# Attention units with one gate each: a gate's copies behind the next scores, ranking from unit 19, matmuls of ones moved

## The chip, the cores and the metric

The kernel runs on one core of a Trainium2 chip. The time is device time in microseconds (us) of one execution. The kernel before was run three times: median 845.96 us, lowest 845.76, highest 846.55. One execution was profiled; it took 846.0 us, of which the profile's span is 844.2.

Engines are called by the profile's names: PE (TensorE) for matmuls and PEld for its loads of weights, DVE (VectorE), ACT (ScalarE), POOL (GpSimd), and SP (SyncE), which issues most transfers.

## What is computed

Three layers follow each other. Attention over 4 x 8 heads of 576 positions and 64 columns, where the first four heads see the last 32 positions and the other four every fourth of the last 128. Then a mixture of 8 experts over the 2304 tokens, of which each token takes two, chosen by noisy gates. Then a last layer shared by all tokens.

```python
scores = scale * np.matmul(q, k.transpose(0, 1, 3, 2))
attn = softmax(np.where(masks, scores, -1e9))
x = np.matmul(attn, v)                                   # 2304 x 512
logits = x @ w_gate
noisy_logits = logits + np.log1p(np.exp(x @ w_noise)) * noise
top2 = the two largest of noisy_logits, weights by their softmax
out[mask] += top2_w * (np.maximum(x[mask] @ w1[e], 0) @ w2[e])
h = out @ w_in;  solu = h * softmax(h)
return (layer_norm(solu) * g_ln) @ w_out
```

## The kernel before

**Attention in units.** The attention is cut into 24 units (NG), numbered s. Unit s belongs to pair p = s // 3 of heads, and t = s % 3 is its third of the positions. A unit handles two pairs of heads, h = 0 and 1, with three blocks each. The work of one unit's group passes through five functions:

- scores(s), lines 168 and 175: on PE the mask and then the products of queries and keys into two banks of PSUM, tags "s" and "t", of two buffers each.
- soft_a(s), lines 184 to 188: on DVE the negative maxima (tile ng), on ACT six exponentials (tile p) that also give the sums.
- soft_b(s), lines 195 to 199: on DVE one over the sums (tile r), on POOL the scaled p (tile pn).
- ptrans(s), lines 208 to 212: on PE six transposes of pn into PSUM of tag "p" (two buffers, one for each h), and copies to SBUF (tile ptS). The copy of h = 0 is ACT's; that of h = 1 is DVE's while s is below PD = 12, then ACT's too.
- pv(s), line 227: on PE the products with v (tag "v", one buffer). What it returns, evac (lines 233 and 236), copies the result on DVE to xt, the transposed input of the next layer.

**The loop over units** (lines 842 to 897) writes the order of every engine's queue by hand, because each engine runs its instructions in the order in which they are issued here. Unit s issues, in this order: the left-over copies of the unit before (`late`), soft_a(s + 1), soft_b(s), the copies of pv(s - 3), scores(s + 2), loads of keys and queries, ptrans(s - 1), pv(s - 2), the loads of v, what `fill` holds for this unit, the gates of this unit, a piece of the splitting of weights (a cast on ACT, line 508, and a difference on POOL, line 511), and a piece of the routing of tokens.

**Gates.** gate(n), lines 258 to 279, takes 128 tokens of xt. On PE it transposes them back to rows and computes their logits in the same matmuls (line 262), into PSUM ga_a and ga_b, which both have tag "p" and so take both of its buffers (or "s" and "t" where it is told so). It returns evac: on DVE the sum of the logits (lines 273 and 274, tile ga), on ACT two copies of the rows (lines 275 and 276, tile xo), and a store of the rows to DRAM (xs, line 277, on SP's queue). GS says which gates a unit has; GE does it for units 24 and 25. The copies of gates 5, 7, 9 and 11 are issued at once, those of the others go to `late` and are issued first in the next unit. A gate can only run when its tokens' xt is complete. Gates 16 and 17 stand behind the loop.

**Routing.** front(s0, n0, n1) computes on DVE, with one exponential on ACT (line 299), the noisy logits of tokens' tiles n0 to n1 and the two largest. rank(n0, n1, ...) counts by matmuls how many tokens come ahead for an expert (lines 343 and 345), and from these builds the lists of tokens of each expert: wide tables (tile hot, line 391 on DVE, multiplied on POOL at line 393), small tables (line 399 on DVE), and matmuls of both into ixp (line 404). From ixp comes idx (lines 411 and 412), and then `then()` is called: early() gathers the first expert's tokens (line 524, an indirect transfer that POOL issues).

front and rank are generators. They yield a planner's cost in nanoseconds after each piece, and wait in the list bg:

```python
    at(FA, lambda: bg.append(front(0, 0, 4)))
    at(FB, lambda: bg.extend((front(0, 4, N1), rank(0, N1, 9, 3, early))))
    at(FC, lambda: bg.append(front(N1, N1, N2)))
```

Up to unit FB - 1 each unit takes three pieces. From FB to unit 23 it takes pieces up to PT = 2000 ns by the planner's costs (a negative cost ends it). Behind the loop come gates 16 and 17, pieces up to 740 ns, the copies of these two gates, and then drain(), which issues all that is left. Only then the transposes of the gathered rows (xtrans, line 541) and the first expert's matmuls (l1, line 554) follow.

**Matmuls of ones.** heat(n), lines 837 to 840, issues n matmuls of a tile of ones whose result nobody reads, into a buffer of tag "p".

Of the kernel before, what the change touches and what calls it, by code (L numbers as in the profile page):

```python
# [34 lines left out]
H0, H1 = 34, 20  # L35
# [4 lines left out]
M1 = 1  # L40
SH = 17
M2 = 6
GS = {8: (0,), 9: (1,), 10: (2,), 11: (3,), 14: (5, 6), 15: (7, 8), 16: (4,), 20: (9, 10), 21: (11, 12)}
FA, FB, FC = 12, 17, 22
WP, WG = (8, 9, 10), 11
CEV = True
GE = (((13, "p", "p"), (14, "s", "t")), ((15, "s", "t"),))
# [59 lines left out]
def tile_kernel(ctx, tc, kq, vw, gates_w, noise, w1, w2, w_in, w_out, g_ln, masks, cpack, out, stop=None):  # L107
# [39 lines left out]
    def load_kq(j, u0=0, u1=S):  # L147
        o = j * 128 * 2 * S
        dst = KQ[j % 4][:, W:].rearrange("p (a s) -> p a s", a=2)[:, :, u0:u1]
        nc.sync.dma_start(dst, dram_ap(kq, o + u0, [[2 * S, 128], [S, 2], [1, u1 - u0]]))  # L150

    def load_v(b, d):
        o = (2 * b + d) * 64 * NBLK * 4 * D
        nc.sync.dma_start(VW[d][W:].rearrange("p i h d -> p (i h d)"),
                          dram_ap(vw, o, [[NBLK * 4 * D, 64], [1, NBLK * 4 * D]]))
# [6 lines left out]
    def scores(s):  # L162
        p, t = divmod(s, 3)
        ps = [psum.tile([128, 3, 96], F32, name="s", tag="st"[h]) for h in range(2)]
        half = [slice(64 * h, 64 * h + 64) for h in range(2)]
        for l in half:
            for h, hd in enumerate(half):
                nc.tensor.matmul(ps[h][l], idb[hd, hd], mk[hd, p % 2, 3 * t:3 * t + 3, :], start=True, stop=False,
                                 skip_group_check=True)
        for i in range(3):  # L170
            u = 64 * (3 * t + i)
            for c, l in enumerate(half):
                j = (2 * p + c) % 4
                for h, hd in enumerate(half):
                    nc.tensor.matmul(ps[h][l, i], QT[j][hd, u:u + 64], KT[j][hd, u:u + 96], start=False,
                                     stop=i == 2, skip_group_check=True)
        G[s] = {"s": ps}

    def soft_a(s):
        ng = work.tile([128, 2, 3], F32, name="ng", bufs=3)  # L180
        p = work.tile([128, 2, 3, 96], F32, name="p", bufs=2)
        sm = work.tile([128, 2, 3], F32, name="sm", bufs=3)
        for h in range(2):
            nc.vector.tensor_reduce(out=ng[:, h], in_=G[s]["s"][h], axis=AX.X, op=OP.max, negate=True)  # L184
        nc.vector.tensor_scalar(ng, ng, scale, None, op0=OP.mult)
        for h in range(2):
            for i in range(3):
                nc.scalar.activation(p[:, h, i], G[s]["s"][h][:, i], AF.Exp, scale=scale, bias=ng[:, h, i:i + 1],  # L188
                                     accum_out=sm[:, h, i:i + 1])
        G[s].update(p=p, sm=sm)  # L190

    def soft_b(s):
        p = G[s]["p"]
        r = work.tile([128, 2, 3], F32, name="r", bufs=3)
        nc.vector.tensor_scalar(r, G[s]["sm"], 1e-9, None, op0=OP.add)  # L195
        nc.vector.reciprocal(r, r)
        pn = work.tile([128, 2, 3, 96], F32, name="pn", bufs=2)
        for h in range(2):
            nc.gpsimd.tensor_tensor(pn[:, h], p[:, h], r[:, h, :, None].to_broadcast([128, 3, 96]), op=OP.mult)
        G[s]["pn"] = pn  # L200

    def ptrans(s):
        pn = G[s]["pn"]
        t = work.tile([96, 2, 3, 128], F32, name="ptS", bufs=2)
        for h in range(2):
            ps = psum.tile([96, 3, 128], F32, name="pt", tag="p")
            for i in range(3):
                nc.tensor.transpose(ps[:, i], pn[:, h, i], idf)
            if h and s < PD:
                nc.vector.tensor_copy(t[:, h], ps)  # L210
            else:
                nc.scalar.copy(t[:, h], ps)
        G[s]["pt"] = t

    def pv(s):
        p, t = divmod(s, 3)
        b, k = divmod(p, 2)
        pt = G[s]["pt"]
        if b not in XT:
            XT[b] = big.tile([128, 4, S], F32, name="xt", tag="xt", bufs=2)  # L220
        x = XT[b][:, 2 * k:2 * k + 2]
        full = psum.tile([128, 512], F32, name="pv", tag="v", bufs=1)
        ps = full[:, :384].rearrange("p (c u) -> p c u", c=2)
        for c in range(2):
            for i in range(3):
                for h in range(2):
                    nc.tensor.matmul(ps[64 * h:64 * h + 64, c, 64 * i:64 * i + 64], VW[k][:, 3 * t + i, 2 * c + h, :],  # L227
                                     pt[:, h, i, 64 * c:64 * c + 64], start=True, stop=True, skip_group_check=True)
        del G[s]

        def evac():
            if k:
                nc.vector.tensor_copy(x[:, :, 192 * t:192 * t + 192], ps)
                return
            for c in range(2):
                nc.vector.tensor_copy(x[:, c].rearrange("p (c i) -> p c i", c=DIL)[:, :, 48 * t:48 * t + 48],
                                      ps[:, c].rearrange("p (i c) -> p c i", c=DIL))

        return evac
# [24 lines left out]
    def gate(n, ta="p", tb="p"):  # L264
        pa = psum.tile([128, 3, 144], F32, name="ga_a", tag=ta)
        pb = psum.tile([128, 1, 144], F32, name="ga_b", tag=tb)
        gate_mm(n, 0, 3, pa)
        gate_mm(n, 3, 4, pb)

        def evac():  # L270
            xo = work.tile([128, DM], F32, name="xo", tag="y", bufs=3)
            t = work.tile([128, 16], F32, name="gt")
            nc.vector.reduce_sum(t, pa[:, :, 128:].rearrange("p k e -> p e k"), axis=AX.X)
            nc.vector.tensor_add(ga[:, n], t, pb[:, 0, 128:])
            nc.scalar.copy(xo[:, :384].rearrange("p (k d) -> p k d", k=3), pa[:, :, :128])
            nc.scalar.copy(xo[:, 384:], pb[:, 0, :128])
            nc.sync.dma_start(xs[128 * n:128 * n + 128], xo)

        return evac
# [472 lines left out]
    def pump(n=1):  # L752
        t = 0
        for _ in range(n):
            while bg:
                try:
                    t = next(bg[0]) or 0
                    break
                except StopIteration:
                    bg.pop(0)  # L760
        return t

    def pump_t(t, stop=False):
        while bg and t > 0:
            c = pump()
            t -= abs(c)
            if stop and c < 0:
                break
        return t
# [67 lines left out]
    def heat(n):  # L837
        ps = psum.tile([128, 128], F32, name="heat", tag="p")
        for _ in range(n):
            nc.tensor.matmul(ps, one, one, start=True, stop=True, skip_group_check=True)  # L840

    heat(H0)
    scores(0)
    soft_a(0)
    scores(1)
    heat(H1)
    late = []
    debt = 0
    for s in range(NG + 2):
        p, t = divmod(s, 3)  # L850
        for f in late:
            f()
        late = []
        if s + 1 < NG:
            soft_a(s + 1)
        if s < NG:
            soft_b(s)
        if s > 2:
            pve()
        if s == 1:  # L860
            ptrans(0)
        if s + 2 < NG:
            scores(s + 2)
        if s == 0:
            heat(H1)
        if t == 0 and p + 2 < 8:
            load_kq(2 * p + 4)
            load_kq(2 * p + 5)
        if 1 < s <= NG:
            ptrans(s - 1)  # L870
        if s > 1:
            pve = pv(s - 2)
            if s == NG + 1:
                pve()
        b, k = divmod(s - 5, 6)
        if s > 4 and k % 3 == 0 and b < 3:
            load_v(b + 1, k // 3)
        for f, a in fill.get(s, []):
            f(*a)
        tiles = [(n,) for n in GS.get(s, ())] + (list(GE[s - NG]) if s >= NG else [])  # L880
        for a in tiles:
            f = gate(*a)
            if a[0] in (5, 7, 9, 11):
                f()
            else:
                late.append(f)
        if s >= WG and first:
            try:
                next(first[0])
            except StopIteration:  # L890
                first.pop(0)
        if FB <= s < NG:
            debt = pump_t(PT + min(debt, 0), True)
        elif s < FB:
            pump(3)
    for h in late:
        h()
    late = [gate(16), gate(17, "s", "t")]
# [222 lines left out]
```

## Time and profile before

| | |
|---|---|
| median of three runs | 845.96 us (845.76 to 846.55) |
| the profiled execution | 846.0 us, span 844.2 us, mean granted clock 0.967 |
| PE busy | 794.4 us, 94% of the span |
| PEld busy | 697.7 us, 83% |
| DVE busy | 519.1 us, 61% |
| ACT busy | 322.7 us, 38% |
| POOL busy | 194.5 us, 23% |

A granted clock of 1.00 is 2.4 GHz on PE, and 0.50 is 1.2 GHz. A mean between them belongs to a stretch that had both. Idle time in front of an instruction is given with what ended it ("<-").

### The profile page before, as it was taken

How to read it: one execution, taken by the hardware profiler on the slowest of the kernel's cores; microseconds unless marked ns; L12 is line 12 of the kernel's file. 1: busy time of each engine (PE TensorE's matmuls, PEld its weight loads, DVE VectorE, ACT ScalarE, POOL GpSimd, SP SyncE). 2: the span in 40 equal slices, each digit the busy share in tenths (PEclk: the TensorE clock that was granted, in tenths of full speed). 3: DMA queues.
4: the chain of work that ended last, by engine and by line, in shares of the span. 5: the costliest groups of instructions: out<-in, count | busy, mean ns of one | idle time of the engine just before them, and what ended most of it. 6: DMA issues, size and time to landing. Idle time of an engine off the chain costs nothing.

```text
span 844.2 us, 14236 instructions
## 1 busy us (share of the span) xinstructions
PE 794.4 (94%) x5470; PEld 697.7 (83%) x5470; DVE 519.1 (61%) x1213; ACT 322.7 (38%) x821; POOL 194.5 (23%) x202
## 2 busy tenths in 40 slices
PE   6977766799999999999999999999999999999997
PEld 5766656798988989989989889899887888888886
DVE  3865576535655845755757554432566777877783
ACT  4877633233322433323223323332434443344332
POOL 3664551812011011010010110022224312322200
PEclk8999757899999999999999999999999999999999
DMA  7666213336336445455264463352422222212101
GB/s 258 215 229 216 88 51 114 112 106 191 119 125 192 158 156 169 150 175 179 97 200 150 137 193 107 118 156 67 145 76 77 67 70 75 63 51 76 38 25 41
DMA packets 56729, 106.21 MB, mean 126 GB/s; under 512 B 6096, under 2 KB 26576, under 8 KB 56144
## 3 DMA queue, kind: packets, MB, share of 16 engines
q1 hardware_dynamic: 50576, 85.31, 31.0%
q0 software_dynamic: 6080, 19.93, 8.0%
q8 instruction: 45, 0.74, 0.4%
q14 instruction: 28, 0.23, 0.1%
HBM read 81.03 MB, written 24.19 MB: 125 GB/s over the span
## 4 chain that ended last, share of the span: by engine, by line
PE 82%; DVE 6%; ACT 1%; DMA 1%; issue 1%; POOL 0%; DVEq 0%; ACTq 0%
PE l L554 53%; PE fh L688 12%; PE fo L554 11%; PE xtp L541 2%; PE fzp L706 2%; PE ga_a L262 1%; DVE hot L399 1%; PE xtp L626 1%; DVE hot L391 1%; ACT p L188 1%; DMA xg<-xs,idx 1%; DVE ng L184 1%; PE ixp L404 0%; PE pv L227 0%; DVE r L195 0%
## 5 line engine op out<-in xcount | busy, mean ns | idle before, releaser
L524 POOL DMA_INDIRECT xg<-xs,idx x40 | 46.2, 1154 | 338.3 <-PE xtp L541 326.0
L554 PE MATMUL l<-x,w1h 128*128 128x256 f32 x512 | 96.8, 287 | 0.8 <-ACT x L545 0.7
L554 PE MATMUL l<-x1h,w1h 128*128 128x384 f32 x256 | 85.9, 335 | 0.0
L554 PEld LDWEIGHTS l<-x,w1h 128*128 128x128 f32 x512 | 84.1, 195 | 2.1 <-ACT x L545 1.1
L554 PE MATMUL l<-x1l,w1h 128*128 128x384 f32 x256 | 85.8, 335 | 0.0
L554 PE MATMUL l<-x1h,w1l 128*128 128x384 f32 x256 | 85.6, 334 | 0.0
L554 PE MATMUL l<-w2h,h1h 128*128 128x512 f32 x192 | 76.8, 400 | 0.0
L554 PE MATMUL l<-w2h,h1l 128*128 128x512 f32 x192 | 75.1, 391 | 0.0
L554 PE MATMUL l<-w2l,h1h 128*128 128x512 f32 x192 | 74.9, 390 | 0.0
L554 PE MATMUL l<-x,w1l 128*128 128x256 f32 x256 | 73.5, 287 | 0.0
L575 DVE SCALAR_TENSOR_TENSOR h1l<-l,h1h 128x384 fp32r<-128x384 f32 x64 | 35.4, 553 | 46.9 <-ACT h1h L574 46.6
L574 ACT ACTIVATE h1h<-l 128x384 fp32r<-128x384 f32 x64 | 31.5, 493 | 83.2 <-PE l L554 81.6
L511 DVE TENSOR_TENSOR w1l<-raw,w1h 128x1024 fp32r<-128x1024 f32 x32 | 38.3, 1230 | 28.2 <-ACT w1h L508 28.2
L600 DVE COPY yo<-l 128x512 f32<-128x512 f32 x22 | 15.2, 691 | 64.6 <-PE l L554 64.6
L188 ACT ACTIVATE p<-s,ng 128x96 f32<-128x96 f32 x144 | 47.0, 345 | 18.6 <-DVE r L195 18.4
L554 PE MATMUL fo<-w2x,fz 128*128 128x512 f32 (+1 forms) x228 | 52.8, 379 | 0.0
L554 PE MATMUL l<-w2h,h0h 128*128 128x512 f32 x128 | 51.9, 405 | 0.0
L554 PE MATMUL l<-w2h,h0l 128*128 128x512 f32 x128 | 51.1, 399 | 0.0
L554 PE MATMUL l<-w2l,h0h 128*128 128x512 f32 x128 | 50.9, 398 | 0.0
L598 ACT COPY yo<-l 128x512 f32<-128x512 f32 x18 | 10.6, 588 | 104.3 <-PE l L554 100.7
L688 PE MATMUL fh<-w1h,fx 128*128 128x512 f32 x144 | 49.1, 403 | 1.2 <-ACT fx L632 0.7
L620 POOL TENSOR_TENSOR yg<-yg 128x512 f32<-128x512 f32 x18 | 23.3, 1293 | 116.2 <-ACT yg L619 116.2
(198 smaller groups left out, 1921.8 us busy)
## 6 DMA issues: line engine op xcount, KB each, us to landing
raw<-in_moe_w_dram SPq DMA_DIRECT2D x64, 512.0 KB
ys<-yo SPq DMA_DIRECT2D x40, 256.0 KB
kq<-in_kq_dram SPq DMA_DIRECT2D x14, 576.0 KB
vwt<-in_vw_dram SPq DMA_DIRECT2D x8, 576.0 KB
xs<-xo SPq DMA_DIRECT2D x18, 256.0 KB
out_dram<-yo SPq DMA_DIRECT2D x17, 256.0 KB
raw<-in_moe_w_in_dram SPq DMA_DIRECT2D x8, 512.0 KB
raw<-in_moe_w_out_dram SPq DMA_DIRECT2D x8, 512.0 KB
```

Source lines behind the costliest of these rows:

```text
L188: nc.scalar.activation(p[:, h, i], G[s]["s"][h][:, i], AF.Exp, scale=scale, bias=ng[:, h, i:i + 1], accum_out=sm[:, h, i:i + 1])
L511: (eng or nc.vector).tensor_sub(l, r, h.bitcast(F32))
L524: nc.gpsimd.indirect_dma_start(out=t, out_offset=None, in_=xs[:128 * N1] if h == 0 else xs, in_offset=bass.IndirectOffsetOnAxis(ap=idx[:, ...
L541: nc.tensor.transpose(ps[:, kk], t[:, 128 * kk:128 * kk + 128], idf)
L554: nc.tensor.matmul(ps, A[x], Bm[y], start=first and i == 0, stop=last and i == 2)
L574: nc.scalar.activation(hh[:, ft], ps, AF.Relu)
L575: nc.vector.scalar_tensor_tensor(hl[:, ft], ps, 0.0, hh[:, ft].bitcast(F32), op0=OP.max, op1=OP.subtract)
L598: nc.scalar.copy(y, ps)
L600: nc.vector.tensor_copy(y, ps)
L620: nc.gpsimd.tensor_tensor(a, a, b, op=OP.add)
L688: nc.tensor.matmul(ps, FX[n][x][:, kk], W1[y][:, 2 * c:2 * c + 2, kk], start=kk == 0 and i == 0, stop=kk == 3 and i == 2)
L706: nc.tensor.transpose(ps[:, kk], u[:, c, 128 * kk:128 * kk + 128], idf)
```

## The change

GS gives every unit from 14 to 18 and from 20 to 23 one gate, where four units had two; gate 4 moves from unit 16 to unit 18. FA, FB and FC, the units at which the pieces of the routing enter the list, move from 12, 17 and 22 to 13, 19 and 24. All copies of gates go to `late`, and `late` is issued behind scores(s + 2) instead of at the head of the unit. Of the three sets of matmuls of ones the second one moves ahead of scores(1), and the third, in unit 0, goes.

```diff
-GS = {8: (0,), 9: (1,), 10: (2,), 11: (3,), 14: (5, 6), 15: (7, 8), 16: (4,), 20: (9, 10), 21: (11, 12)}
-FA, FB, FC = 12, 17, 22
+GS = {8: (0,), 9: (1,), 10: (2,), 11: (3,), 14: (5,), 15: (6,), 16: (7,), 17: (8,), 18: (4,), 20: (9,), 21: (10,), 22: (11,),
+      23: (12,)}
+FA, FB, FC = 13, 19, 24
...
     heat(H0)
     scores(0)
     soft_a(0)
+    heat(H1)
     scores(1)
-    heat(H1)
     late = []
     debt = 0
     for s in range(NG + 2):
         p, t = divmod(s, 3)
-        for f in late:
-            f()
-        late = []
         if s + 1 < NG:
             soft_a(s + 1)
...
         if s + 2 < NG:
             scores(s + 2)
-        if s == 0:
-            heat(H1)
+        for f in late:
+            f()
+        late = []
...
         for a in tiles:
             f = gate(*a)
-            if a[0] in (5, 7, 9, 11):
-                f()
-            else:
-                late.append(f)
+            late.append(f)
```

## Rows read from the trace of the kernel before

**Rows 1.** Stretches: start:end, us, busy of each engine (instructions), granted clock, DMA share, GB/s.

```profile
11.04:13.63 2.59, 2.59 (x40) 2.36 (x40) 1.06 (x4) 0.00 (x1) 0.00 (x0) 0.50 1.03 421
40.74:58.54 17.80, 14.18 (x259) 11.40 (x256) 11.27 (x39) 12.69 (x62) 9.52 (x12) 1.00 0.86 286
58.54:61.42 2.88, 1.94 (x53) 1.55 (x53) 2.75 (x9) 2.78 (x15) 2.37 (x4) 1.00 0.00 0
61.42:93.48 32.06, 22.61 (x396) 18.10 (x394) 22.45 (x102) 22.16 (x100) 18.16 (x21) 0.99 0.46 150
83.47:93.48 10.01, 5.81 (x119) 4.28 (x117) 9.47 (x40) 6.15 (x31) 7.16 (x8) 0.96 0.16 49
93.48:109.99 16.51, 12.73 (x128) 11.12 (x129) 7.20 (x36) 9.42 (x40) 4.88 (x6) 0.71 0.32 115
109.99:132.44 22.45, 16.42 (x188) 14.22 (x187) 14.53 (x31) 7.76 (x26) 11.60 (x10) 0.63 0.26 75
132.44:140.70 8.26, 2.80 (x17) 2.00 (x16) 5.89 (x39) 2.50 (x7) 2.10 (x2) 0.77 0.60 188
140.70:844.20 703.50, 691.56 (x3798) 612.26 (x3798) 431.47 (x883) 240.20 (x444) 126.06 (x113) 0.99 0.37 116
```

**Rows 2.** Order of time, unit 10: start, us, engine, line, what, count, idle and releaser.

```profile
40.74 0.34 ACT L188 ACTIVATE p<-s,ng 128x96 f32<-128x96 f32 x1 [0.63 <-DVE r L195]
...
42.66 0.48 ACT L212 COPY ptS<-pt 96x384 f32<-96x384 f32 x1
...
43.39 0.21 DVE L273 TENSOR_REDUCE gt<-ga_a 128x16 f32<-128x48 f32 x1 [1.48 <-PE ga_a L262]
...
43.83 0.81 DVE L184 TENSOR_REDUCE ng<-s 128x3 f32<-128x288 f32 x2
...
44.95 0.34 ACT L188 ACTIVATE p<-s,ng 128x96 f32<-128x96 f32 x1 [0.67 <-DVE r L195]
```

**Rows 3.** Order of time, unit 2 to 3: transposes, DVE's copy, next maxima.

```profile
19.43 0.86 PE L208 MATMUL pt<-cp,pn 128*96 128x128 f32 x6
...
20.33 0.55 DVE L210 COPY ptS<-pt 96x384 f32<-96x384 f32 x1 [0.67 <-PE pt L208]
...
20.81 0.81 DVE L184 TENSOR_REDUCE ng<-s 128x3 f32<-128x288 f32 x2
```

**Rows 4.** Order of time, unit 14 to 15: two gates.

```profile
65.15 0.48 ACT L275 COPY xo<-ga_a 128x384 f32<-128x384 f32 x1 [0.96 <-DVE gt L273]
...
65.69 1.00 PE L262 MATMUL ga_a<-wg,xt 128*128 128x144 f32 x6 [0.56 <-ACT xo L275]
...
66.86 0.32 PE L168 MATMUL s<-mk 64*64 64x288 bf16 x4
```

**Rows 5.** Order of time, unit 12 to 13: first front's exponential read, then pv.

```profile
56.45 1.07 DVE L301 TENSOR_SCALAR rw<-ru 128x32 f32<-128x32 f32 x1 [1.36 <-ACT ru L299]
...
59.23 0.92 PE L227 MATMUL pv<-ptS,vwt 96*64 96x64 f32 x24 [2.17 <-DVE xt L233]
```

**Rows 6.** Order of time, unit 20: pv behind the second front.

```profile
94.18 1.55 PE L227 MATMUL pv<-ptS,vwt 96*64 96x64 f32 x24 [3.06 <-DVE xt L233]
```

**Rows 7.** Lines 391 and 399 (min/median/max ns), then the index in order of time.

```profile
L391 DVE TENSOR_TENSOR hot<-cp,pbi x5: 642/1335/1735, 111.1 to 157.2; 128x288 f16<-128x288 f32 x3, 128x720 f16<-128x720 f32 x2
...
L399 DVE TENSOR_TENSOR hot<-cp,pbi x9: 344/901/1415, 114.0 to 160.4; 128x192 f16<-128x192 f32 x6, 128x384 f16<-128x384 f32 x3
...
121.12 1.43 PE L404 MATMUL ixp<-hot 128*64 128x40 f16 x24 [0.99 <-DVE hot L399]
...
131.75 0.19 DVE L411 TENSOR_SCALAR ix<-ixp 128x40 f32<-128x40 f32 x1
```

**Rows 8.** Order of time, units 0 and 1: scores 1, ones, group 2's exponentials.

```profile
11.04 0.46 PE L168 MATMUL s<-mk 64*64 64x288 bf16 x4 [5.16 <-DMA mk<-in_masks_dram]
...
12.39 2.08 PE L840 MATMUL heat<-one 128*128 128x128 bf16 x20
...
16.59 0.34 ACT L188 ACTIVATE p<-s,ng 128x96 f32<-128x96 f32 x1 [0.92 <-DVE r L195]
```

## The prediction

> **What bounds the kernel now.** I read the table of stretches first, then the instructions in order of time inside the stretches that stood out, then the single lines of the ranking. I cut the stretches at the first exponential of a group of scores: group g's exponentials are issued in unit g-1, so group 10's stand in unit 9. In [rows 1] the 703.50 us from 140.70 on have TensorE busy for 691.56 of them: the experts and the last layer are TensorE's own, and the change touches nothing there. Everything it touches lies ahead of that, where no engine is full. There I call the time from one group's first exponential to the next group's a round; a round without a gate is 2.88 us (58.54 to 61.42 [rows 1]).
>
> Why a round with a gate is longer shows in [rows 2]: exponentials at 40.74, the copy of the transposes at 42.66 (1.92 later), DVE's read of the gate at 43.39 after 1.48 us idle for its matmuls, and only then the next maxima at 43.83 (0.44 later) and the next exponentials at 44.95. The gate's reads stand ahead of the next group's maxima on DVE and of its exponentials on ACT, so one round takes 4.21 us. Two gates in a unit are worse: the second one's matmuls start 0.54 us after the first one's copy does [rows 4].
>
> **The change, part by part.** All sums are against the profiled execution, 846.0 us (span 844.2 and 1.8 around it), 0.04 above the median of the runs shown.
>
> *Matmuls of ones.* TensorE's queue holds 34 at the start, 20 between scores 1 and scores 2, and 20 more behind those; after the change 34, and 20 where TensorE waits anyway (5.16 us idle before scores 1 [rows 8]). So scores 2 no longer stand behind 2.08 us of ones. Group 2's exponentials start at 16.59; ACT is through with group 1's at 13.63 + 1.92 = 15.55 (13.63 is a cut of [rows 1]), so at most 1.0 is gained. The other bound is a loss: scores 1 run at 1.2 GHz now, and with nothing behind them the clock may stay there for the next two units; doubling the 0.86 us of a set of transposes [rows 3] is the nearest price, and half of it hidden gives 0.4 lost. I take 0.2 gained. From 11.04 to 13.63 the granted clock is 0.50, 1.2 GHz [rows 1], after those 5.16 us without a matmul. The Trainium skill (TensorE: Matmul & The Clock Gate, "Why this matters for your kernels") tells kernels to leave no idle gaps between bursts of matmuls, or the rate halves. By that rule, with which this row agrees, the moved ones, which end well ahead of scores 1, would not save the clock; the 0.2 would be a loss and the sum 0.4 higher.
>
> *Copies behind the next scores, gates 0 to 3.* Round 9 to 10 loses its gate (4.21 to 2.88); unit 8's copy to xstr stays in DVE's queue ahead of the next maxima, so I take 1.1 of the 1.33. The next four rounds get a new loop. A gate's two results take both banks of tag "p", which the next transposes want. Those now wait for the copies, the copies stand behind the exponentials on ACT, and up to PD = 12 the second copy of the transposes is DVE's, ahead of the next maxima in its queue. The loop: maxima to exponentials 1.12 (43.83 to 44.95 [rows 2]), exponentials 1.92, copy of the gate to TensorE 0.54 [rows 4], transposes to DVE's copy 0.90, that copy to the next maxima 0.48 [rows 3]; together 4.96, where it was 4.21. Four of them are 19.84; from group 10 to 14 it was 17.80 [rows 1]. That is 2.0 lost.
>
> *The first front, one unit later.* Its first exponential on ACT makes DVE wait, and the maxima behind it. Before, that is in round 13 to 14: 17.80 less three rounds of 4.21 and one of 2.88 leaves 2.29; the reading of ACT's result took 1.07 us on DVE at 56.45 [rows 5]. It moves to round 14 to 15, which was 2.88: 2.3 lost there (what it cost before is inside the 17.80). Up to group 15, then, 1.1 gained and 4.3 lost: **3.2 lost**.
>
> *One gate a unit, gates 5, 6, 7, 8, 4.* Groups 15 to 21 took 32.06 us [rows 1]. Now there is one round without a gate (3.5: 2.88 and something for the second half of xstr in unit 14) and five with one. The copy of h = 1 is ACT's there, so DVE is out of the loop, and the round's lower bound is ACT's own: 1.92 + 0.54 + 0.90 + 0.48 for the last copy = 3.84. The upper bound is the loop above, 4.96. I take the middle, 4.4, because ACT also has a cast of a weight in most of these units. 3.5 + 22.0 = 25.5: **6.6 gained**. TensorE needs about 3.65 a round (0.7 for scores, half of the 1.35 from 11.04 to 12.39 at half rate [rows 8]; 0.86 for transposes, 0.92 for pv, 1.17 for a gate from 65.69 to 66.86 [rows 3 to 5]), so it nearly fills it.
>
> *Groups 21 to 23.* These held two units of two gates at half clock: 16.51 us at a mean clock of 0.71. The planner's numbers put into these two units (20 and 21) the same eight and nine steps of the front that units 18 and 19 have now, and those took 10.01 us [rows 1] with no gates. One gate's read on DVE (0.44 [rows 2]) comes on top: 10.4, **6.1 gained**.
>
> *From group 23 to the first gather.* This is 22.45 us now, with the tables for the index (lines 391, 399) inside, at a mean clock of 0.63 [rows 1]. Ranking begins two units later, so by the planner's costs unit 23 gets as far as unit 21 did, and the tables fall behind the last gates: one in the step of 740 ns before gates 16 and 17 are read, the rest in drain(). TensorE's list before that: three sets of transposes, four of pv, gates 11 to 15: 3 x 0.86 + 4 x 0.92 + 5 x 1.17 = 12.1 us at full clock. It starts 2.5 us after group 23's exponentials do (1.92 + 0.54), and I add 1.5 for waits on copies: 16.1. In the round before that, TensorE waits some 3 us for DVE's front, as it did at 94.18 (3.06 us idle, and pv then took 1.55 instead of 0.92 [rows 6]); so I expect 1.2 GHz for a stretch here and add 2.5 (bounds 0 and 5.1; the 16.51 us at 0.71 hold 9.6 us at half rate, which lose 4.8). So 18.6. Then gates 16 and 17, 2.3, and their read, 0.4; the second wide table 1.3 (line 391's median); six small ones; the last 24 index matmuls 1.4; from ix to the gather 0.7 (131.75 to 132.44) [rows 1, 7]. A small table took 0.34 to 1.42, median 0.90 [rows 7]; POOL, which had transposes' inputs and weights to make beside them, has little more than its multiplications now, so I take 0.55 (3.3; bounds 2.1 and 5.4). In sum 28.0: **5.6 lost**. Here row and rule can be weighed: the row only shows the spread. The Trainium skill (SBUF — State Buffer, "Who interferes with whom") says that DVE with two operands in SBUF and a reading POOL hold a shared port by turns for a whole instruction. By it four of the six would run bare, at 0.34, and the sum be about 0.8 lower.
>
> *Behind it.* The 8.26 us from gather to the experts' first matmul, and all after that, carry over. DMA queues: SP gets the same transfers in the same order; a store of a gate stands ahead of kq's loads as before, 2 us later, and those have four units to land. POOL's order is the same but for the tables' multiplications, which move ahead of the first gather; priced above.
>
> Sum: -0.2 + 3.2 - 6.6 - 6.1 + 5.6 = -4.1, so **841.9 us**.
>
> **The rivals.** *A, the clock holds after group 22* and POOL leaves the tables alone: 2.5 and 1.2 less, 838.2. For it: gates no longer come in pairs. Against it: the front's steps are the same, and they starved TensorE before [rows 6].
>
> *B, the loop through the two banks everywhere.* If a round costs the whole loop also in units 15 to 19, because TensorE, let go late by the banks, has the next scores late, five rounds cost 4.96 (2.8 more), and gates 10 to 12 0.55 each: 4.4 more, 846.3, no change. The change then doesn't do what it says: the wait for a gate is moved to the banks, not removed. For it: TensorE's 3.65 leaves little slack. Against: ACT makes both copies there, so DVE's maxima needn't wait for the transposes.
>
> *C, the clock falls at unit 13's wait.* Round 14 to 15 is 5.2 us with 2.5 of TensorE's work (3.65 less a gate), so it waits 2.7. Before, a wait of 2.17 in such a round left the clock at 1.00 [rows 1, 5], and one of 3.06 stands where pv next ran slow [rows 6]; 2.7 lies between. Rounds of 7.3 (twice 3.65) then replace 4.4 for as long as it lasts. Over 9.6 us at half rate that is 1.3 rounds in place of 2.2, 3.8 lost, no change in all; over 16.6 (as in the 22.45 at 0.63) it is 6.6 lost, **848.5**, slower. It decides from about 15 us on.
>
> **How the numbers follow.** A difference under 0.2% (1.7 us) can't be told from no change. Chances: the forecast 0.51 (839.5 to 844.2), A 0.19, B 0.14, C 0.16. So faster 0.70, same 0.14, slower 0.16. The range is 836.5 to 848.5: low end A with rounds near 3.84, high end C's whole price.
>
> **What would show it.** Right: exponentials of groups 17 to 21 some 4.4 us apart; groups 10 to 14 about 5.0 apart, with DVE's copy of h = 1 just ahead of the maxima; group 23 near 99; lines 391 and 399 behind the last gate, TensorE idle beside them; first gather near 127, experts' first matmul near 136. Wrong: rounds of 5 in units 15 to 19, a stretch at 1.2 GHz around 65 to 85, or an index table that takes over 6 us.

## The result, and the profile after

The changed kernel took 838.22 us (median of four runs, 837.50 to 839.57) beside 845.86 us for the kernel before in the same job (four runs, 843.23 to 846.55): a ratio of 0.9917, 95% interval 0.9893 to 0.9942. That is 7.6 us faster by the medians. The forecast was 841.9, 4.1 faster.

The profiled execution of the changed kernel took 839.57 us, the longest of its four; its span is 837.8. The two profiled spans differ by 6.4 us, and this is the difference that can be followed from stretch to stretch. The lines of the kernel quoted here stand one higher in the changed kernel than before. First the stretches, cut at the same events as in [rows 1] (columns: start:end, us, busy of PE, PEld, DVE, ACT and POOL with their instructions, granted clock, DMA share, GB/s):

```profile
39.04:59.82 20.78, 15.60 (x287) 13.15 (x280) 10.26 (x39) 13.28 (x62) 9.52 (x12) 0.92 0.64 212
59.82:64.99 5.17, 3.33 (x64) 2.44 (x61) 3.25 (x8) 2.90 (x16) 3.58 (x4) 1.00 0.51 184
64.99:90.89 25.90, 22.16 (x370) 18.77 (x374) 20.68 (x77) 21.77 (x100) 15.85 (x20) 0.87 0.55 185
90.89:100.62 9.73, 6.77 (x125) 5.78 (x118) 9.08 (x43) 7.24 (x32) 6.05 (x7) 0.96 0.44 143
100.62:127.34 26.72, 20.66 (x229) 17.92 (x227) 15.37 (x56) 11.08 (x37) 10.25 (x10) 0.76 0.34 119
127.34:134.26 6.92, 2.18 (x9) 1.44 (x9) 5.36 (x35) 1.40 (x3) 2.10 (x2) 0.50 0.31 81
134.26:837.80 703.54, 691.59 (x3798) 612.22 (x3798) 431.59 (x883) 239.78 (x444) 125.92 (x113) 0.99 0.36 116
```

| stretch | before | after | difference | forecast |
|---|---|---|---|---|
| start to group 10 | 40.74 | 39.04 | -1.70 | -1.3 |
| groups 10 to 14 | 17.80 | 20.78 | +2.98 | +2.0 |
| groups 14 to 15 | 2.88 | 5.17 | +2.29 | +2.3 |
| groups 15 to 21 | 32.06 | 25.90 | -6.16 | -6.6 |
| groups 21 to 23 | 16.51 | 9.73 | -6.78 | -6.1 |
| group 23 to the first gather | 22.45 | 26.72 | +4.27 | +5.6 |
| gather to the experts' first matmul | 8.26 | 6.92 | -1.34 | 0 |
| from there to the end | 703.50 | 703.54 | +0.04 | 0 |
| sum | 844.20 | 837.80 | -6.40 | -4.1 |

What was gained, 12.9 us in the units that had two gates, was partly given back in three places. Each can be seen.

**Given back: rounds 10 to 14.** The order of time in one such round of the changed kernel (start, us, engine, line, operation, tile, count, idle before and what ended it):

```profile
54.62 0.34 ACT L189 ACTIVATE p<-s,ng 128x96 f32<-128x96 f32 x1 [0.86 <-DVE r L196]
...
56.54 0.50 ACT L276 COPY xo<-ga_a 128x384 f32<-128x384 f32 x1
...
57.18 0.83 PE L209 MATMUL pt<-cp,pn 128*96 128x128 f32 x6 [1.41 <-ACT xo L276]
...
58.05 0.55 DVE L211 COPY ptS<-pt 96x384 f32<-96x384 f32 x1 [2.39 <-PE pt L209]
...
58.53 0.81 DVE L185 TENSOR_REDUCE ng<-s 128x3 f32<-128x288 f32 x2
...
59.82 0.34 ACT L189 ACTIVATE p<-s,ng 128x96 f32<-128x96 f32 x1 [1.05 <-DVE r L196]
```

Read it as a chain. The copy of the gate stands behind the exponentials (54.62 to 56.54), TensorE's transposes wait for it (57.18, released by xo), DVE's copy waits for the transposes (58.05, after 2.39 us idle), the maxima stand behind that copy (58.53), and the next exponentials behind them. One turn is 5.20 us where [rows 2] had 4.21. Over the attention units the view of tile xo's waiters has "PE pt L209" 11 times, 12.8 us in all.

**Given back: the first front's wait**, in round 14 to 15:

```profile
62.47 0.26 ACT L300 ACTIVATE ru<-ra 128x32 f32<-128x32 f32 x1
...
62.76 1.21 DVE L302 TENSOR_SCALAR rw<-ru 128x32 f32<-128x32 f32 x1 [1.85 <-ACT ru L300]
...
64.99 0.34 ACT L189 ACTIVATE p<-s,ng 128x96 f32<-128x96 f32 x1 [2.27 <-DVE r L196]
...
65.68 1.12 PE L228 MATMUL pv<-ptS,vwt 96*64 96x64 f32 x16 [2.16 <-DVE xt L234]
```

DVE waits 1.85 us for one small exponential, the maxima wait behind it, and TensorE then waits 2.16 us (the last row shows 16 of this pv's 24 matmuls). What follows is the low clock of rival C, for a short time: 0.60 from 64.99 to 73.44, then 1.00 to 90.89.

**Gained: one gate a unit.** A round of the changed kernel with the gate's copies and both copies of the transposes on ACT:

```profile
77.55 0.34 ACT L189 ACTIVATE p<-s,ng 128x96 f32<-128x96 f32 x1
...
79.46 0.50 ACT L276 COPY xo<-ga_a 128x384 f32<-128x384 f32 x1
...
79.75 0.80 DVE L185 TENSOR_REDUCE ng<-s 128x3 f32<-128x288 f32 x2
...
80.11 0.83 PE L209 MATMUL pt<-cp,pn 128*96 128x128 f32 x6 [0.53 <-ACT xo L276]
...
80.71 0.85 ACT L213 COPY ptS<-pt 96x384 f32<-96x384 f32 x2 [0.57 <-PE pt L209]
...
81.45 0.62 ACT L509 CAST w1h<-raw 128x512 fp32r<-128x512 f32 x1
...
81.97 0.34 ACT L189 ACTIVATE p<-s,ng 128x96 f32<-128x96 f32 x1
```

Here DVE's maxima start at 79.75, long before they are needed. ACT sets the round: exponentials 1.91, the gate's copies and the wait for the transposes 1.25 (79.46 to 80.71), their copies 0.74, the cast of a weight 0.52; together 4.42. The rounds from group 17 to 21 are 4.11, 4.42, 4.41 and 4.51. Before, the two rounds between groups 21 and 23, with two gates each and more than half of the time at the low clock, hold 16.51 us [rows 1]. The other two rounds with two gates, groups 15 to 17 of the kernel before, ran at a granted clock of 1.00 and took 6.83 and 6.82 us. So the pair of gates is dear without the low clock too; up to 2.9 of the 16.51 us go with the front's waits and the low clock, which no run takes apart.

**Given back: the tables behind the last gates.** From the last gates to the experts:

```profile
121.20 1.38 DVE L392 TENSOR_TENSOR hot<-cp,pbi 128x720 f16<-128x720 f32 x1
...
122.51 2.88 DVE L400 TENSOR_TENSOR hot<-cp,pbi 128x192 f16<-128x192 f32 x6
122.67 1.44 POOL L394 TENSOR_TENSOR hot<-hot,cp 128x720 f16<-128x720 f16 x1 [0.84 <-DVE hot L392]
...
124.37 2.24 PE L405 MATMUL ixp<-hot 128*64 128x40 f16 x33 [1.20 <-DVE hot L400]
...
126.65 0.20 DVE L412 TENSOR_SCALAR ix<-ixp 128x40 f32<-128x40 f32 x1 [1.17 <-PE ixp L405]
...
127.34 1.16 POOL L525 DMA_INDIRECT xg<-xs,idx  x1 [3.24 <-DVE ef L419]
...
131.08 1.09 PE L542 MATMUL xtp<-cp,xg 128*128 128x128 f32 x4 [4.47 <-DMA xg<-xs,idx]
...
132.49 1.09 PE L542 MATMUL xtp<-cp,xg 128*128 128x128 f32 x4 [0.32 <-DMA xg<-xs,idx]
```

From 121.01, when gates 16 and 17 have left TensorE, to 127.34 it has nothing to do but the index.

### The profile page after: what moved, and what is told of

Read it like the earlier page. It is cut to its first block, busy times and chain, and to the rows that moved or that the text cites. A ratio compares the mean times of both kernels' runs of the same rounds, so it can differ in the third digit from the quotient of the medians.

```text
span 837.8 us, 14196 instructions
## 1 busy us (share of the span) xinstructions
PE 793.7 (95%) x5450; PEld 697.8 (83%) x5450; DVE 519.3 (62%) x1213; ACT 321.7 (38%) x821; POOL 193.0 (23%) x202
## 4 chain that ended last, share of the span: by engine, by line
PE 87%; DVE 6%; ACT 3%; DMA 1%; issue 1%; SPq 1%; POOL 0%; DVEq 0%; ACTq 0%
PE l L555 53%; PE fh L689 12%; PE fo L555 11%; ACT p L189 3%; PE xtp L542 2%; PE fzp L707 2%; PE pt L209 2%; PE ga_a L263 1%; DVE ng L185 1%; DMA mk<-in_masks_dram 1%; PE pv L228 1%; PE xtp L627 1%; PE s L176 1%; DVE hot L400 1%; DVE hot L392 1%
```

## The experiments

Ten kernels ran, each timed in five rounds against the kernel before on the same chip. "Experts" is the start of the experts' first matmul in the profile; behind it the ten profiles and the two above take 701.9 to 703.6 us whatever the kernel, so a single profile is best compared there. Two kernels of one job can be compared by their medians. The changed kernel ran in another job than the ten: the kernel before had a median of 845.86 us there and of 844.03, 844.43 and 844.96 in the jobs of e1 to e4, e5 to e8, and e9 and e10. So a difference of 1 or 2 us from the changed kernel is given by the ratios too (times 845 us).

| kernel | median us (range, runs) | ratio to before (95%) | experts |
|---|---|---|---|
| before | 845.86 (843.23 to 846.55, 4) | | 140.70 |
| changed | 838.22 (837.50 to 839.57, 4) | 0.9917 (0.9893 to 0.9942) | 134.26 |
| e1_heat_back | 838.15 (836.49 to 839.77, 6) | 0.9924 (0.9907 to 0.9942) | 134.37 |
| e2_copies_first | 837.55 (835.69 to 838.64, 6) | 0.9914 (0.9896 to 0.9931) | 133.53 |
| e3_pd8 | 835.89 (834.67 to 837.03, 5) | 0.9895 (0.9878 to 0.9911) | 131.66 |
| e4_stop | 836.65 (834.37 to 839.41, 6) | 0.9905 (0.9884 to 0.9926) | 132.41 |
| e5_tables_24 | 835.16 (833.49 to 835.26, 5) | 0.9885 (0.9868 to 0.9903) | 128.13 |
| e6_before_rank19 | 843.25 (841.29 to 844.36, 12) | 0.9980 (0.9968 to 0.9991) | 137.88 |
| e7_all | 829.67 (827.60 to 831.46, 5) | 0.9818 (0.9796 to 0.9839) | 126.17 |
| e8_hybrid | 828.90 (827.84 to 830.12, 5) | 0.9810 (0.9793 to 0.9827) | 125.08 |
| e9_hybrid_heat | 828.63 (826.13 to 830.06, 5) | 0.9795 (0.9774 to 0.9816) | 124.01 |
| e10_no_heat1 | 840.55 (837.62 to 841.44, 6) | 0.9933 (0.9914 to 0.9952) | 136.34 |

### The matmuls of ones put back (e1_heat_back)

```diff
     soft_a(0)
-    heat(H1)
     scores(1)
+    heat(H1)
...
             scores(s + 2)
+        if s == 0:
+            heat(H1)
```

> The changed kernel with its matmuls of ones put back as before (20 behind scores 1, 20 behind scores 2). My theory, that the order of gates makes the gain and the head next to nothing: 838.0 to 839.2 us, group 2's exponentials later by up to 1.0 us against the start of scores 1, rounds from group 9 on as in the changed kernel. Rival, that the moved matmuls of ones keep TensorE's clock up and make much of the gain: 840 us or more, with a clock of 0.5 for longer up to group 10.

838.15 beside 838.22 (by the ratios 0.6 more): no difference that can be told. The rounds from group 10 to 14 are 5.01, 5.02, 5.01 and 5.23, at a granted clock of 1.00, and the transposes and pv in them take 0.83 and 0.92 us each time. So the longer rounds are not the clock's doing, and the rival, 840 us or more, falls: much of the gain is not in the order of the ones. Less than about 2 us of it isn't excluded by the intervals.

### The copies back at the head of the unit (e2_copies_first)

```diff
         p, t = divmod(s, 3)
+        for f in late:
+            f()
+        late = []
...
             scores(s + 2)
-        for f in late:
-            f()
-        late = []
```

> The changed kernel with the gates' copies back at the head of the unit, still one gate a unit. My theory, that behind the exponentials the copies cost rounds 10 to 14 (5.2 us where they were 4.2) and save in rounds 16 to 23: rounds 10 to 13 back at 4.2 (3 us gained), rounds of gates from 16 on near 5.0 (the one single gate with ACT making both copies took 5.0 before; 3 to 4 us lost), in sum 838 to 840. Rival, that the order of the copies is the whole gain: 844 to 846.

837.55, no slower than the changed kernel, and far from the rival's 844 to 846. From group 10 to 13 the old order is faster, 4.19 a round against 5.0 to 5.6 (round 9 to 10 is slower, 4.86 against 3.67). Behind group 16 it is slower: 5.29, 5.00, 5.30 and 4.99 where the changed kernel has 5.29, 4.11, 4.42 and 4.41; only the last round to group 21, left without a gate's copies by the old order, is shorter, 2.94 against 4.51. In sum groups 9 to 14 take 20.32 us here and 24.45 in the changed kernel, groups 14 to 21 34.51 and 31.07, groups 21 to 23 10.87 and 9.73. One such round of this kernel, in order of time:

```profile
71.68 0.34 ACT L189 ACTIVATE p<-s,ng 128x96 f32<-128x96 f32 x1 [0.63 <-DVE r L196]
...
74.12 1.00 PE L263 MATMUL ga_a<-wg,xt 128*128 128x144 f32 x6 [0.76 <-ACT ptS L213]
...
75.16 0.21 DVE L274 TENSOR_REDUCE gt<-ga_a 128x16 f32<-128x48 f32 x1 [0.67 <-PE ga_a L263]
...
75.56 0.82 DVE L185 TENSOR_REDUCE ng<-s 128x3 f32<-128x288 f32 x2
...
76.68 0.34 ACT L189 ACTIVATE p<-s,ng 128x96 f32<-128x96 f32 x1 [0.63 <-DVE r L196]
```

The gate waits for the copies of the transposes, which hold its banks (74.12); DVE reads it ahead of the maxima (75.16, 75.56). So each order has its own loop. Where the copy of h = 1 is DVE's, the old loop of 4.19 is the shorter one; where both copies are ACT's, the new order is, 4.4 against 5.0. Over the attention the two balance (65.70 and 65.25 us from group 9 to 23), so the order of the copies is not the gain of the whole change. That is left to what this kernel keeps: one gate a unit, with the later ranking (e6).

### Both copies of the transposes on ACT from unit 8 (e3_pd8)

```diff
-PD = 12
+PD = 8
```

> The changed kernel with PD = 8 in place of 12: ACT, not DVE, makes the copy of the second half of the transposes in units 9 to 12. My theory, that these rounds are a loop through that copy in DVE's queue: rounds 10 to 14 fall from about 5.2 to 4.2 to 4.6, 835.5 to 836.5 us. Rival, that the wait for the two banks of tag p sets the round whoever makes the copy: rounds stay at 5.0 and the time at 838.2.

835.89, 2.3 less than the changed kernel, and 2.3 less than e1 of the same job (1.9 by the ratios, whose intervals overlap). Groups 10 to 14 take 17.83 us in place of 20.78, or of e1's 20.27. Their rounds are 3.90, 5.12, 4.40 and 4.41; the second, at a mean granted clock of 0.67, lies outside the 4.2 to 4.6 expected. A round at the full clock:

```profile
47.59 0.35 ACT L189 ACTIVATE p<-s,ng 128x96 f32<-128x96 f32 x1
...
49.91 0.82 DVE L185 TENSOR_REDUCE ng<-s 128x3 f32<-128x288 f32 x2 [0.52 <-PE s L176]
50.13 0.83 PE L209 MATMUL pt<-cp,pn 128*96 128x128 f32 x6 [0.29 <-ACT xo L276]
...
51.99 0.34 ACT L189 ACTIVATE p<-s,ng 128x96 f32<-128x96 f32 x1
```

The maxima (49.91) now come before the transposes (50.13), and what they wait for is their scores. The round is 4.40, ACT's own bound as in units 17 to 19. The loop through DVE's copy is confirmed.

### A waiting piece ends the unit's share (e4_stop)

```diff
         elif s < FB:
-            pump(3)
+            for _ in range(3):
+                if pump() < 0:
+                    break
```

> The changed kernel where a piece of the first front that waits for ACT ends the unit's share (as it does from unit 19 on), so that DVE's read of ACT's exponential stands in the next unit. My theory, that round 14 to 15 holds a 2.3 us stall of DVE behind that exponential: that round falls from 5.2 to 3.0 to 3.4 and the time to 836.0 to 836.8 us. Rival, that the stall only moves to the next unit, where DVE is as short of time: 838.0.

836.65, 1.6 less (1.0 by the ratios, whose intervals overlap): the time alone doesn't show a gain, the round does. The front's pieces with a negative cost, which wait for ACT, now end a unit's share ahead of FB too, as they already did behind it. In order of time around group 15 of this kernel:

```profile
60.21 0.81 DVE L185 TENSOR_REDUCE ng<-s 128x3 f32<-128x288 f32 x2
...
61.85 0.25 ACT L300 ACTIVATE ru<-ra 128x32 f32<-128x32 f32 x1
62.09 0.34 ACT L189 ACTIVATE p<-s,ng 128x96 f32<-128x96 f32 x1
...
63.38 0.64 DVE L302 TENSOR_SCALAR rw<-ru 128x32 f32<-128x32 f32 x1
```

The maxima (60.21) precede the exponential (61.85), and DVE reads it a unit later without waiting. Round 14 to 15 is 2.89 in place of 5.17, and the granted clock is 1.00 from 62.09 to 87.35. In e1, e3 and e10, which keep the wait (2.15, 2.21 and 2.17 us), it is 0.59 to 0.60 from group 15 to 17, as in the changed kernel, and in e5 (2.17 us) 0.78. So in these kernels the wait of TensorE at this place and the lower clock behind it go together.

### The tables also in units 24 and 25 (e5_tables_24)

```diff
-        if FB <= s < NG:
+        if FB <= s < NG + 2:
             debt = pump_t(PT + min(debt, 0), True)
```

> The changed kernel that also lets units 24 and 25 take pieces of the ranking (2000 ns each by the planner's costs), so that the tables of the index stand beside the last gates in place of behind them. My theory, that the tables behind the last gates cost the 4.3 us that group 23 to the first gather got longer: the gather comes 2 to 4 us earlier and the time is 834.5 to 836.5 us, although the copies of gates 13 to 15 are then late. Rival, that DVE's tables only push those copies and pv back by as much: 837.5 to 838.5.

835.16, 3.1 less (2.7 by the ratios). The order of time in this kernel:

```profile
111.27 1.73 DVE L392 TENSOR_TENSOR hot<-cp,pbi 128x720 f16<-128x720 f32 x2
...
112.91 1.55 DVE L400 TENSOR_TENSOR hot<-cp,pbi 128x192 f16<-128x192 f32 x1
...
117.04 1.42 DVE L400 TENSOR_TENSOR hot<-cp,pbi 128x192 f16<-128x192 f32 x5
...
120.00 1.15 POOL L525 DMA_INDIRECT xg<-xs,idx  x1 [3.06 <-DVE ef L419]
...
126.37 1.08 PE L542 MATMUL xtp<-cp,xg 128*128 128x128 f32 x4 [1.70 <-DMA xg<-xs,idx]
```

The tables stand among the last transposes and gates, and the gather starts 21.4 us after group 23 (98.59) in place of 26.7. Of these 5.3 us 1.2 are given back: from the gather to the experts it is 8.13 us again, not 6.92. The second gather's rows come 4.90 us after its issue at 121.47 here, 3.68 in the changed kernel (128.81 to 132.49).

### Later ranking alone, in the kernel before (e6_before_rank19)

```diff
-FA, FB, FC = 12, 17, 22
+FA, FB, FC = 13, 19, 24
```

> The kernel before with the later routing alone (FA, FB, FC = 13, 19, 24), two gates in a unit, copies and matmuls of ones as before. My theory, that one gate a unit is the gain and the later ranking a loss by itself: 845 to 850 us, units 15, 16, 20 and 21 still 6 to 9 us long. Rival, that the later ranking makes the gain by leaving DVE free for the gates: 841 us or less.

843.25, a ratio of 0.9980: a small gain where a loss was expected, and far from 841. Its rounds with two gates remain (columns as for the stretches above; one of the four):

```profile
59.46:68.06 8.60, 7.37 (x73) 6.44 (x74) 3.57 (x14) 4.71 (x20) 1.34 (x2) 0.60 0.47 162
```

The other three are 6.81, 7.78 and 7.73. Kernel e2 differs from this one in the spread of the gates, in the copies of gates 5, 7, 9 and 11, which this one issues at once and e2 a unit later, and in the ones, which bring nothing that e1 shows. The two ratios, 0.9914 over 0.9980, give 0.9934: about 5.6 of the 7.3 us (0.0086 of 845) go with the spread of the gates, give or take some 2 us by the intervals, and about 1.7 with the later ranking. That spread with ranking from unit 17 as before wasn't tried: gate 4 stands in unit 18, and the pieces from FB on read it.

### Three mendings together, and the better order in each part (e7_all, e8_hybrid)

e7 is e3, e4 and e5 in one. e8 keeps e4 and e5, leaves PD at 12, and puts each copy where its loop is the shorter one:

```diff
         p, t = divmod(s, 3)
+        if s < 14:
+            for f in late:
+                f()
+            late = []
```

> The changed kernel with three of the edits together: PD = 8, a piece that waits for ACT ends the unit's share, and pieces of the ranking in units 24 and 25. If the three cost separate stretches, their gains add: 2.3 and 1.6 measured and 2 to 4 expected, 830.5 to 832.5 us. If they share the same slack, 834 or more.

> The same three edits, but PD = 12 and the copies of gates 0 to 3 at the head of the unit as before, those of the other gates behind the next scores. My theory: rounds 10 to 13 at 4.2, rounds 16 to 21 at 4.1 to 4.5, each order where it is the shorter one, 830 to 832 us, within 1 us of the same with PD = 8. Rival, that mixing the orders costs a round where they meet, in unit 14: 833 or more.

e7 took 829.67 and e8 828.90, both below the ranges expected. The three gains alone add to 7.0 us (2.3 + 1.6 + 3.1); together they are 8.5 (5.6 and 8.4 by the ratios). So none is seen to take from another; what they are together above their sum is within the spread of the runs. The intervals of the ratios of e7 and e8 overlap: which of the two is faster isn't shown. In e8 rounds 10 to 13 are 4.19 as expected; of those from group 16 to 21, 4.42, 4.81, 4.42, 4.40 and 5.43, two lie outside the 4.1 to 4.5 expected. Two of its stretches (columns as above), groups 10 to 14 and group 23 to the gather:

```profile
40.15:55.61 15.46, 13.32 (x253) 10.86 (x252) 10.35 (x37) 12.49 (x60) 8.29 (x12) 1.00 0.88 288
...
95.21:116.69 21.48, 18.54 (x220) 16.14 (x220) 14.62 (x52) 9.77 (x33) 10.84 (x11) 0.80 0.31 106
```

The first was 20.78 us in the changed kernel, the second 26.72. Both kernels beat the changed kernel by about 9 us, and the kernel before, in their own job, by about 15 (14.8 and 15.5).

### The ones again (e9_hybrid_heat, e10_no_heat1)

e9 is e8 with e1's edit. e10 is the changed kernel with the edit

```diff
     soft_a(0)
-    heat(H1)
     scores(1)
```

> Asks what the place of the matmuls of ones is worth on top of the best version (828.90 us). Theory: nothing that the clock can show, because group 9's first exponential stood at 34.06 to 35.87 in all profiles with either order, and the order before in the changed kernel gave 838.15 beside 838.22; so 828.4 to 829.4. Rival: ones behind scores 1 hold TensorE at the full clock through units 1 to 3 (mean granted clock up to group 9 of 0.99 and 1.00 in the two profiles that have them there, 0.79 and 0.93 in two that have not), and this is worth the time between: group 9 near 34.5 in place of 35.27, 828.0 to 828.3, with no stretch under 0.98 from group 1 to group 9.

> The changed kernel without the one set of matmuls of ones that it keeps between the first two units' scores: only the 34 at the start are left. Theory (this set does little where it stands, since TensorE falls to half rate behind it anyway): 838.0 to 838.8. Rival (it holds the clock for scores 1, which took 0.69 us at full rate in the changed kernel and 1.22 where the set stands behind them): scores 1 at half rate and a longer stretch at half rate behind them, 0.5 to 2 us more at group 9, 838.9 to 840.5.

e9 took 828.63 beside 828.90: again no difference that can be told. The time can't part the theory from the rival, whose ranges lie 0.1 us apart where the runs spread over 4. The rival's mark didn't come: group 9 stood at 36.12, not 34.5, and the granted clock from group 1 to 2 was 0.63. But the second mask of scores, which ends TensorE's wait before scores 1, landed 1.03 us later here than in e8; from that landing to group 9 it is 25.49 us here and 25.67 in e8. e10 took 840.55, 2.3 above the changed kernel (1.4 by the ratios) and above the theory's range, but its range overlaps the other's and the intervals of the ratios do too. Nor does its profile show a loss where the rival put it: group 9 came at 34.68 (35.37 in the changed kernel), and the time was lost behind group 22. Whether this set of ones is worth anything stays open.

## Why the prediction came out as it did

The direction held, and so did the mechanisms of the middle stretches; the gain was 2.3 us larger than the sum in the profiled execution, and the rest of the 3.7 between 841.9 and 838.22 is the run: the profiled one was 1.35 above its median. The misses cancel in part: rounds 10 to 14 and groups 15 to 21 cost 1.0 and 0.4 more than forecast, the start 0.4 and groups 21 to 23 0.7 less, the way to the first gather 1.3 less and that from it to the experts another 1.3 less. The median lies inside the range, but below the 839.5 to 844.2 that the forecast itself had been given.

**Matmuls of ones**, 0.2 gained: the times show nothing either way (e1, e9). What happened in the head is the landing of the second mask. It ended TensorE's wait before scores 1 at 11.04 in the profile of before, at 9.21 in e6, which has the same head, at 10.63 in e9, and at 9.04 in the changed kernel. So the first row of the table, 1.70 gained where 1.3 were forecast, is luck: the landing alone came 2.00 earlier, and from it to group 10 the changed kernel took 30.00 us and the kernel before 29.70. The term itself looks like a loss there: from the landing to group 9 it is 26.33 us in the changed kernel, and 24.83 and 24.85 in the kernel before and e6. But e8 and e9, which differ in the ones alone, are 0.2 apart, so the size stays open. The mean granted clock from group 1 to 9 was 0.79 in the changed kernel, and 0.99 in e6. The Trainium skill (TensorE: Matmul & The Clock Gate, "Why this matters for your kernels") says to leave no gaps between bursts of matmuls. These two clocks agree with it in sign, but not at the place that the prediction had: scores 1 ran at the full rate in the changed kernel (their products took 0.69 us, 1.22 in e1), and the low clock, 0.50, came behind them, from 12.94 to 18.82.

**Round 9 to 10**, 1.1 gained: 4.87 became 3.67, so 1.2.

**The new loop**, 4.96 a round and 2.0 lost: this was the mechanism, shown by e3. The rounds were 5.56, 5.01, 5.01 and 5.20. The step that fell short is the clock, which the sum held at 1.00 here; in the profile it was 0.92, and most of the missing 0.9 is in the first round, whose transposes took 1.38 us (at 41.60) in place of 0.86 and whose pv took 1.55. In e1, at 1.00, the four took 20.27.

**The first front**, 2.3 lost: 2.29, and e4 takes it back.

**One gate a unit**, 4.4 a round and 6.6 gained: 4.4 held from group 17 on, and its reason too, that ACT is the bound there, though the number itself was only the middle of two bounds. The 0.4 missing lies in round 16 to 17, 5.29 us in the low clock behind 65.68. That is rival C's event, priced at 3.8 to 6.6; groups 15 to 17 took 8.45 us with it and 8.02 at 1.00 in e4, though the front's read has moved behind group 15 there. So rival C's event did come, after a wait of 2.16 us, but it was too short to decide.

**Groups 21 to 23**, 6.1 gained: 6.78. The 9.73 us are what units with the same steps of the front and no gates had taken (10.01), so one gate's 0.44 costs nothing visible. The low clock of the old stretch (0.71) was not in the new one (0.96), as the forecast had it.

**From group 23 to the gather**, 28.0: 26.72. TensorE came to gates 16 and 17 after 18.15 us (100.62 to 118.77; forecast 18.6), they took 2.24 (2.3), the wide table 1.38 (1.3), the six small ones 2.88 (3.3), from there to ix 1.26 (1.4), and 0.69 to the gather (0.7). The largest misses are TensorE's list and the small tables, 0.45 and 0.42. Five of the six tables took 345 or 346 ns and one 1,542, and this one lies beside POOL's 1.44 us at 122.67. The prediction's spread, median 0.90, came from nine instructions of two widths [rows 7]. The Trainium skill (SBUF — State Buffer, "Who interferes with whom") has DVE with two operands in SBUF and a reading POOL hold one port by turns for a whole instruction. The trace agrees in kind: one table is long beside POOL, and the others are bare, five where I had said four. The sum that I drew from it, 0.8 lower, took 0.55 for those that POOL holds, and the held one took 1.54; so it comes out as far from 2.88 on one side as my 3.3 on the other.

**Behind it**, "carry over": this is the step that was wrong, a term put at nothing. The 8.26 us became 6.92. In both kernels the first gather's rows took 3.7 to 3.8 us from issue to transposes (132.44 to 136.27, 127.34 to 131.08). The second one's took 5.02 before:

```profile
133.92 0.94 POOL L524 DMA_INDIRECT xg<-xs,idx  x1 [0.32 <-issue]
...
138.94 1.09 PE L541 MATMUL xtp<-cp,xg 128*128 128x128 f32 x4 [2.04 <-DMA xg<-xs,idx]
```

and 3.68 after, 1.34 less, which is the whole difference. In the kernel before, a load of a weight (512 KB) was issued at 129.71 and three stores of rows (256 KB each) between 132 and 135 us, and 188 GB/s were moved up to the experts; in the changed kernel, between 126 and 136 us, only a store of 36 KB was, and 81 GB/s were moved. Where the gather stands among those stores again, as in e5, e7, e8 and e9 (172, 177, 175 and 193 GB/s), the stretch is 8.13, 8.22, 8.39 and 8.20 us. In the other six kernels of the experiments it is 6.86 to 6.99 us, 6.99 at 80 GB/s in e6, whose gates and copies are those of the kernel before. So in all twelve profiles long gathers and other transfers go together; no run took the transfers alone away. I had counted what each queue is moved past, not what is in flight beside the gather.

**The rivals.** A gave 838.2, which is the median, but that is luck, as it got there by another way: after group 22 the clock did not hold (0.76 from group 23 to the gather, TensorE's list 18.15 of the 18.6 forecast), and only its cleaner tables came in part. B's loop through the banks does not rule the rounds from group 17 to 21 (4.11 to 4.51, not 4.96).

Of the marks named ahead, the first gather stood at 127.34 (forecast 127), group 23 at 100.62 (99), and the experts' first matmul at 134.26 (136).

## What to carry to other kernels

When an engine's instruction is moved back in a hand-written order, follow the buffer that it frees: the next writer of that buffer now waits for it, and if what that writer feeds stands ahead of the critical work on a third engine, a new loop is made. The same order can be right in one part of a loop and wrong in another (e2 beside the changed kernel: 4.19 and 5.01, then 5.0 and 4.4), depending on which engine holds the last copy. Work that was spread among busy units and slides behind the last of them lengthens the end (4.27 us from group 23 to the gather here; taken back in e5), so spreading one load evenly is worth checking for what it pushes out there. And a stretch at the start that begins with a transfer's landing is best measured from that landing.

## What was not expected of the hardware

- Nearly the same wait of TensorE was followed by very different clocks. After 2.16 us idle at 65.68 in the changed kernel the mean granted clock was 0.60 from 64.99 to 73.44. After 2.17 us in the kernel before it stayed at 1.00 [rows 1, 5]. After 2.61 us idle at 97.93 in the changed kernel the next pv still took its 0.92 us, and only the gate behind it, 1.63 us long at 99.54 in place of 1.00, was slow.
- The landing of the second mask varied by 1.8 us between profiles of kernels whose order up to there is the same (9.21 in e6, 11.04 before), which is as much as most parts of this change are worth.
